# Output blocks stored one by one with the last in the first one's home, activation sums on VectorE only, and layer-norm statistics held until well into the first FFN product

## The chip, the cores and the metric

The kernel runs on one core of one Trainium2 chip. The metric is the device time of one execution in microseconds (us), in the fast state.

Times of one kernel differ by 1 to 2.5 us from execution to execution, once by 5, and much of what is studied here is smaller than that. Beside the time I use one length read from each profiled execution, called **TensorE's stretch** below: from the last attention score matmul ahead of the first steady FFN product (it starts near 33 us) to the start of the kernel's last matmul. It leaves the start-up out.

## The reference, cut to what matters

```python
def _attn_ref(q, k, v):                      # 8 batches, 12 heads, 448 rows, head size 64
    scores = np.matmul(q, k.transpose(0, 1, 3, 2)) / np.sqrt(q.shape[-1])
    attn = np.maximum(scores, 0.0) ** 2 / q.shape[2]
    return np.matmul(attn, v)

def _moe_ref(x, g_ln, w_ch1, w_ch2):         # x: 8 x 448 x 768, inner width 3072
    mu = np.mean(x, axis=-1, keepdims=True)
    var = np.mean((x - mu) ** 2, axis=-1, keepdims=True)
    xn = (x - mu) / np.sqrt(var + 1e-06) * g_ln
    return x + np.maximum(xn @ w_ch1, 0.0) @ w_ch2
```

The attention of a batch comes first; its result x goes through a layer norm and two products with a relu between them.

## The kernel before: the parts that matter

The kernel builds its instruction order itself. `R.add(engines, costs, emit, deps, key)` hands in an operation; where two engines are named, a small model of the chip in the builder gives it to the one that would finish first. The order on each engine is then fixed in the program, and an engine doesn't pass over an instruction that waits: at 490 us of before, ScalarE stood for 1.53 us at a waiting square root while a relu that TensorE needed was behind it. Attention of later batches is laid between FFN matmuls of earlier ones.

Six words for what follows. *ffn_1* is the first FFN product (L929), its relu is L945 on ScalarE or L947 on VectorE. The *second FFN product* of a pair of 128-row tiles is computed from four output blocks (C11, C12 for the first tile, C21, C22 for the second) with seven products P1 to P7 (L1114) instead of eight. These need sums of activations, S1 to S4 (L1074). An *evacuation* (L1128) takes a finished product out of PSUM, multiplies it by 1/std and adds; only then is the PSUM bank free for the next product. *Mean subtraction* (L840) and *gain* (L847 on ScalarE, L849 on VectorE) prepare the input of the next batch's ffn_1.

The activation sums, which the builder may give to VectorE or GpSimd:

```python
def s_op(u, m, name, part, deps):
    ...
    def emit(eng):
        (nc.vector if eng == "DVE" else nc.gpsimd).tensor_sub(o, i0, i1)
    return R.add(("DVE", "POOL"), (540.0, 1700.0), emit, deps, key=-2.9, port=True)
```

`port=True` tells the builder's model that this operation can't run beside one of the other engine that is marked so too. The mean subtraction is not marked:

```python
    subs.append(R.add("DVE", 130.0 + (P if m < 3 else T) * K1 * 1.04,
                      lambda eng, cols=cols, i=i: sub(eng, cols, slice(0, K1), i), [sv], key=-2.0))
```

Evacuations, homes and stores. `e["o", 0]` is a 128 x 768 tile for the first tile's blocks (from two buffers in rotation), `e["o", 1]` a 128 x 384 half tile, of which there is one. `half_free[0]` is the last store out of it:

```python
        if name == "P1":
            evac("c1", 0, lo, r1, False, [o_ring[-N_O]])
        elif name == "P2":
            evac("C11", 0, lo, r1, True, [e["c1"]])
        ...
        elif name == "P5":
            evac("p5", 1, hi, r2, False, [half_free[0]])
        elif name == "P7":
            ev = evac("C22", 1, hi, r2, True, [e["p5"]])
            half_free[0] = store_tile(u, m + 1, hi, ev, False, lambda: e["o", 1])
        elif name == "P3":
            ev = evac("C12", 0, hi, r1, True, [e["c2"], e["C11"]])
            o_ring.append(store_tile(u, m, slice(0, d_model), ev, False, lambda: e["o", 0]))
        else:                                                   # P4
            ev = evac("C21", 1, lo, r2, False, [half_free[0]])
            ...
            half_free[0] = store_tile(u, m + 1, lo, ev, final, lambda: e["o", 1])
```

So C21 needs the half tile that C22 has just used: its evacuation waits for C22's store. Last, the statistics (L790 to L792 on VectorE), their square root on ScalarE (L800) and the reciprocal on VectorE (L802):

```python
            sto = R.add("DVE", 1400.0, stats, [deps_of[m], ops.get(("st0", b))], key=4.0)
        ...
        sq = R.add("ACT", 300.0, root, [ops["st", u, m] for m in ms], key=3.0)
        ops["rstd", b] = R.add("DVE", 150.0, ..., [sq], key=3.0)      # reciprocal
```

## Time and profile before

| | before |
|---|---|
| time, median of 3 | 538.98 us (538.92 to 539.05) |
| span of the profiled execution | 537.3 us |
| TensorE busy | 517.1 us, 96% |
| VectorE / ScalarE / GpSimd busy | 341.8 / 231.3 / 125.2 us |
| TensorE's stretch | 499.43 us |

TensorE is the bound. Two more views belong to the picture. The first is the busy time of each engine in three stretches of before; its columns are the stretch, its length, and for TensorE, its weight loads, VectorE, ScalarE and GpSimd the busy time and the number of instructions; the last three are the clock, the DMA engines' share and GB/s.

```profile
270.00:300.00 30.00, 26.30 (x165) 14.27 (x157) 18.84 (x29) 9.50 (x14) 13.76 (x12) 1.00 1.19 148
400.00:425.00 25.00, 23.20 (x145) 13.01 (x144) 17.15 (x27) 7.46 (x12) 6.11 (x7) 1.00 0.53 107
470.00:500.00 30.00, 29.32 (x162) 15.73 (x161) 9.39 (x23) 10.55 (x20) 1.64 (x1) 1.00 0.24 41
```

The first number after the length is TensorE: it stands still for 3.70, 1.80 and 0.68 us in these three, while it is all but full elsewhere after the start-up. GpSimd is the fifth: it is far busier in the first stretch than its average of 23%.

The durations of the activation sums, by engine (shortest/median/longest in ns, then the first and last start):

```profile
L1074 DVE TENSOR_TENSOR h<-h,x_all x32: 543/550/1561, 199.4 to 524.5; 128x768 bf16<-128x768 bf16 x32
...
L1074 POOL TENSOR_TENSOR h<-h,x_all x4: 1637/1794/1951, 275.5 to 405.7; 128x768 bf16<-128x768 bf16 x4
```

Only four of these 36 run on GpSimd (a fifth sum, of another form, does so at 485.31 us), and two of VectorE's 32 (at 275.97 and 404.59 us) took 1.56 us, almost three times as long as the others. A median alone hides them; the longest tells of them.

### The profile page before, as it was taken

What the parts mean: (1) busy time and instruction counts of PE and PEld (TensorE: products, weight loads), DVE (VectorE), ACT (ScalarE), POOL (GpSimd) and SP (SyncE); (2) the same over time, 40 slices, a digit from 0 to 9 for tenths busy, and PEclk for the clock granted to TensorE, in tenths of its full rate; (3) what the DMA queues carried; (4) which work ended last, traced back from release to release, by engine and by line L of the source; (5) the groups of instructions that cost most, each with busy time, mean ns of one, the idle gap of its engine ahead of it and who ended that gap; (6) DMA issues with size and microseconds to landing.
All of it is one profiled execution on the core that took longest, in us unless ns stands there. A gap on an engine that the chain in (4) does not pass through costs nothing.

```text
span 537.3 us, 9903 instructions
## 1 busy us (share of the span) xinstructions
PE 517.1 (96%) x4128; PEld 278.8 (52%) x4128; DVE 341.8 (64%) x617; ACT 231.3 (43%) x370; POOL 125.2 (23%) x137
## 2 busy tenths in 40 slices
PE   4899999999999999999988999999998999999996
PEld 3444455555564455555544545655555455554564
DVE  5988647448987588665686666746668646633253
ACT  5977611134225653366223663346441565124300
POOL 6411600311460123421172010702222012101000
PEclk9999999999999999999999999999999999999999
DMA  9999999897299004990069900992022400231022
GB/s 187 196 189 195 198 188 165 117 142 134 47 186 187 1 2 68 185 152 1 1 115 159 147 2 1 162 190 52 2 47 71 97 1 1 59 67 23 1 60 59
DMA packets 142680, 51.82 MB, mean 96 GB/s; under 512 B 121510, under 2 KB 139436, under 8 KB 142636
## 3 DMA queue, kind: packets, MB, share of 16 engines
q0 software_dynamic: 81072, 25.50, 45.1%
q1 hardware_dynamic: 55724, 14.79, 17.7%
q10 hardware_dynamic: 5840, 10.92, 7.4%
q8 instruction: 32, 0.52, 0.4%
q14 instruction: 12, 0.10, 0.1%
HBM read 51.91 MB, written 11.01 MB: 117 GB/s over the span
## 4 chain that ended last, share of the span: by engine, by line
PE 90%; DVE 5%; DMA 2%; ACT 1%; issue 1%; SPq 0%; ACTq 0%; DVEq 0%
PE f_ps L929 40%; PE f_ps L1114 20%; PE f_ps L1190 16%; PE sc L586 6%; PE ps L648 5%; DVE a L840 1%; DMA f<-in_k_dram 1%; DVE a L610 1%; DMA out_dram<-o_t 1%; DVE o_t L1128 1%; ACT a L595 1%; PE ps L507 1%; DVE t L365 0%; PE f_ps L909 0%; DVE a L849 0%
## 5 line engine op out<-in xcount | busy, mean ns | idle before, releaser
L929 PE MATMUL f_ps<-a,w 128*128 128x448 bf16 x1134 | 220.9, 353 | 1.8 <-DVE o_t L1128 1.1
L929 PEld LDWEIGHTS <-w 128*128 128x128 bf16 x1134 | 108.3, 98 | 110.3 <-issue 12.5
L595 ACT ACTIVATE a<-sc 128x896 bf16<-128x896 f32 x114 | 99.9, 923 | 85.6 <-PE sc L586 79.8
L945 ACT ACTIVATE h<-f_ps 128x448 bf16<-128x448 f32 (+1 forms) x161 | 86.0, 535 | 103.9 <-PE f_ps L929 102.4
L610 DVE TENSOR_TENSOR a<-a 128x896 bf16<-128x896 bf16 x156 | 99.0, 668 | 3.1 <-ACT a L595 2.8
L1114 PEld LDWEIGHTS <-h 128*128 128x128 bf16 x648 | 62.8, 98 | 48.7 <-issue 7.5
L1114 PE MATMUL f_ps<-w,h 128*128 128x384 bf16 x432 | 75.6, 326 | 4.4 <-DVE o_t L1128 4.4
L597 DVE TENSOR_SCALAR a<-sc 128x896 bf16<-128x896 f32 x45 | 48.9, 1087 | 24.5 <-PE sc L586 24.4
L1190 PE MATMUL f_ps<-w,h 128*128 128x384 bf16 x372 | 62.1, 326 | 0.0
L586 PE MATMUL sc<-t 64*64 64x448 bf16 x672 | 48.4, 365 | 3.3 <-ACT a L595 1.6
L1190 PEld LDWEIGHTS <-h 128*128 128x128 bf16 x372 | 36.0, 98 | 25.2 <-issue 1.7
L739 POOL TENSOR_TENSOR sum_t<-sum_t,xT_all 128x384 f32<-128x384 f32 (+2 forms) x25 | 20.4, 815 | 99.0 <-ACT xT_all L363 99.0
L1074 DVE TENSOR_TENSOR x_all<-h 128x768 bf16<-128x768 bf16 x18 | 9.9, 562 | 38.5 <-ACT h L945 38.5
L1128 DVE SCALAR_TENSOR_TENSOR o_t<-f_ps,r_t,x_all 128x384 f32<-128x384 f32 x36 | 22.1, 615 | 18.8 <-PE f_ps L1114 14.9
L586 PEld LDWEIGHTS <-t 64*64 64x64 bf16 x672 | 17.6, 106 | 26.5 <-issue 20.1
L737 POOL TENSOR_TENSOR sum_t<-xT_all 128x384 f32<-128x384 bf16 (+2 forms) x13 | 9.2, 720 | 88.9 <-ACT xT_all L363 88.8
L648 PE MATMUL ps<-a,v_t 64*64 64x448 bf16 x552 | 29.8, 350 | 0.0
L847 ACT ACTIVATE a<-a,g_sb 128x448 bf16<-128x448 bf16 x27 | 16.1, 657 | 31.2 <-DVE a L840 30.1
L1128 DVE SCALAR_TENSOR_TENSOR o_t<-f_ps,r_t,o_t 128x384 f32<-128x384 f32 x27 | 16.6, 615 | 19.4 <-PE f_ps L1114 19.2
L363 ACT CAST xT_all<-ps 128x768 bf16<-128x768 f32 (+2 forms) x33 | 20.2, 622 | 20.1 <-PE ps L648 18.3
L401 POOL DMA_DIRECT2D t<-in_q_dram x12 | 19.3, 1774 | 36.1 <-DMA t<-t 34.6
L648 PEld LDWEIGHTS <-v_t 64*64 64x64 bf16 x672 | 19.7, 107 | 13.4 <-issue 2.8
(91 smaller groups left out, 420.2 us busy)
## 6 DMA issues: line engine op xcount, KB each, us to landing
out_dram<-o_t ACTq DMA_DIRECT2D x38, 192.0 KB, 4.7
v_t<-in_v_dram POOLq DMA_DIRECT2D x16, 336.0 KB, 6.3
w<-in_moe_w_ch_dram POOLq DMA_DIRECT2D x4, 1152.0 KB, 40.0
t<-in_q_dram POOLq DMA_DIRECT2D x12, 336.0 KB, 8.3
t<-in_k_dram POOLq DMA_DIRECT2D x12, 336.0 KB, 10.5
out_dram<-o_t ACTq DMA_DIRECT2D x35, 96.0 KB, 2.2
w<-in_moe_w_ch_dram POOLq DMA_DIRECT2D x4, 768.0 KB, 19.2
w<-in_moe_w_ch_dram POOLq DMA_DIRECT2D x1, 1536.0 KB, 29.2
```

What stands on the lines that cost most here:

```text
L363: nc.scalar.copy(o, i)
L586: nc.tensor.matmul(sc[rows_of(half), r, :S], qkT[b][rows_of(r), 1, s * NPER + pn, rows_of(half)], qT[:, :, pn, rows_of(half)], start=True, ...
L595: nc.scalar.activation(attn[n, s], st[0][:, :, :S], Act.Relu, scale=rc2)
L597: nc.vector.tensor_scalar(attn[n, s], st[0][:, :, :S], rc2, 0.0, op0=Alu.mult, op1=Alu.max)
L610: nc.vector.tensor_mul(attn[n, s], attn[n, s], attn[n, s])
L648: nc.tensor.matmul(av_st[n][half][rows_of(hh)], vt[b][rows_of(half), 2 * pn + hh, s * D:(s + 1) * D], attn[n, s][rows_of(half), hh, :], st ...
L739: nc.gpsimd.tensor_add(s0, s0, x0)
L929: nc.tensor.matmul(st[0], w1[:, ki, ni * P:(ni + 1) * P], xc[b][:, ki, :], start=(i == 0), stop=(i == K1 - 1))
L945: nc.scalar.activation(o, st[0][:, c], Act.Relu)
L1114: nc.tensor.matmul(e["ps", bank], a(k), w(k), start=new and k == 0, stop=k == KH - 1, skip_group_check=True)
L1128: nc.vector.scalar_tensor_tensor(o, e["ps", bank], r, o if more else xm[u, m + tile_n][:, cols], op0=Alu.mult, op1=Alu.add)
L1190: nc.tensor.matmul(o_st["ps"], stat(u, m, ki), w, start=(i == 0), stop=(i == len(ks) - 1))
```

## The change

It has three parts. The sums are given to VectorE alone. Each output block is stored when it is done, and C21, the last, goes into C11's home in the 128 x 768 tile, which C11's own early store has freed. And for all but the first pair of batches, the statistics wait for the fifth relu of the same batch's ffn_1 (index 4), the square root for the fifteenth (index 14). It is this relu that takes ffn_1 out of PSUM; the recorded texts call it ffn_1's evacuation.

```diff
-            sto = R.add("DVE", 1400.0, stats, [deps_of[m], ops.get(("st0", b))], key=4.0)
+            sto = R.add("DVE", 1400.0, stats, [deps_of[m], ops.get(("st0", b)), later("h", b, 4) if u > 0 else None], key=4.0)
 ...
-        sq = R.add("ACT", 300.0, root, [ops["st", u, m] for m in ms], key=3.0)
+        sq = R.add("ACT", 300.0, root, [ops["st", u, m] for m in ms] + [later("h", b, 14) if u > 0 else None], key=3.0)
 ...
-        return R.add(("DVE", "POOL"), (540.0, 1700.0), emit, deps, key=-2.9, port=True)
+        return R.add("DVE", 570.0, emit, deps, key=-2.9, port=True)
 ...
-                elif key in ("p5", "C21"):
+                elif key == "p5":
 ...
-                o = e["o", 1] if tile_n else e["o", 0][:, cols]
+                o = e["o", 1] if key in ("p5", "C22") else e["o", 0][:, cols]
 ...
-            evac("C11", 0, lo, r1, True, [e["c1"]])
+            ev = evac("C11", 0, lo, r1, True, [e["c1"]])
+            e["C11 out"] = store_tile(u, m, lo, ev, False, lambda: e["o", 0][:, lo])
 ...
-            o_ring.append(store_tile(u, m, slice(0, d_model), ev, False, lambda: e["o", 0]))
+            e["C12 out"] = store_tile(u, m, hi, ev, False, lambda: e["o", 0][:, hi])
 ...
-            ev = evac("C21", 1, lo, r2, False, [half_free[0]])
+            ev = evac("C21", 1, lo, r2, False, [e["C11 out"]])
 ...
-            half_free[0] = store_tile(u, m + 1, lo, ev, final, lambda: e["o", 1])
+            o_ring.append([e["C12 out"], store_tile(u, m + 1, lo, ev, final, lambda: e["o", 0][:, lo])])
```

## The prediction

> **What bounds the kernel now.** I read the page first. Its busy line and the first line of its chain of waits say that TensorE sets the time:
>
> ```profile
> PE 517.1 (96%) x4128; PEld 278.8 (52%) x4128; DVE 341.8 (64%) x617; ACT 231.3 (43%) x370; POOL 125.2 (23%) x137
> PE 90%; DVE 5%; DMA 2%; ACT 1%; issue 1%; SPq 0%; ACTq 0%; DVEq 0%
> ```
>
> The change removes no matmul, so it can only win what TensorE stands still. The second number of the second line is not that amount: the chain runs through VectorE and a store for most of 276 to 293 us, yet TensorE works through much of that stretch. So I went to TensorE's timeline and listed every wait after 30 us (before that, the start-up, the built order of the changed kernel is the same). Five rows carry nearly all of it; the bracket at the end is the idle time before the row and who ended it:
>
> ```profile
> 281.30 2.11 PE L1114 MATMUL f_ps<-w,h 128*128 128x384 bf16 x12 [1.80 <-DVE o_t L1128]
> 286.12 2.11 PE L1114 MATMUL f_ps<-w,h 128*128 128x384 bf16 x12 [0.76 <-DVE o_t L1128]
> 293.25 6.97 PE L929 MATMUL f_ps<-a,w 128*128 128x448 bf16 x36 [1.13 <-DVE o_t L1128]
> ...
> 409.91 2.11 PE L1114 MATMUL f_ps<-w,h 128*128 128x384 bf16 x12 [1.80 <-DVE o_t L1128]
> ...
> 490.95 14.91 PE L929 MATMUL f_ps<-a,w 128*128 128x448 bf16 x78 [0.68 <-ACT h L945]
> ```
>
> Matmul ends are modelled, so I size each by the cadence instead: rows of 12 start 1.95 us apart, 0.1625 us a matmul; the 448-column ones 0.189 us. The row before 281.30 began at 278.84 with three matmuls, so it could have gone on at 279.33: lost 1.97. Likewise 283.24 + 12 x 0.1625 = 285.19 against 286.12: 0.93. 290.80 + 6 x 0.189 = 291.93 against 293.25: 1.32. 407.45 + 3 x 0.1625 = 407.94 against 409.91: 1.97. 477.62 + 66 x 0.189 = 490.09 against 490.95: 0.86. Sum: **7.05 us**. There is one more of 0.32 us at 428.94.
>
> Why VectorE was late: its own timeline and GpSimd's, same stretch.
>
> ```profile
> 275.97 1.56 DVE L1074 TENSOR_TENSOR h<-h,x_all 128x768 bf16<-128x768 bf16 x1
> 277.46 3.25 DVE L840 TENSOR_TENSOR a<-xT_all,sum_t 128x768 bf16<-128x768 bf16 x2
> 280.64 0.60 DVE L1128 SCALAR_TENSOR_TENSOR o_t<-f_ps,r_t,o_t 128x384 f32<-128x384 f32 x1
> ...
> 283.49 2.05 DVE L849 TENSOR_SCALAR a<-a,g_sb 128x448 bf16<-128x448 bf16 x3
> 285.47 0.60 DVE L1128 SCALAR_TENSOR_TENSOR o_t<-f_ps,r_t,x_all 128x384 f32<-128x384 f32 x1
> ...
> 292.58 0.62 DVE L1128 SCALAR_TENSOR_TENSOR o_t<-f_ps,r_t,x_all 128x384 f32<-128x384 f32 x1 [3.69 <-DMA out_dram<-o_t]
> ```
> ```profile
> 275.49 3.55 POOL L1074 TENSOR_TENSOR h<-h,x_all 128x768 bf16<-128x768 bf16 x2 [1.37 <-PE f_ps L1114]
> ```
>
> While GpSimd does two of the four activation sums (L1074), VectorE's own sum takes 1.56 us where its median is 0.55, and one of the two mean subtractions (L840) takes 2.39 where it is 0.95 elsewhere. The evacuation that frees the PSUM bank comes behind them, at 280.64. 404 to 410 us is the same picture (sums 3.55, L840 3.26). Later the gain multiplications (L849) take 2.05 for three, where 0.81 is usual (412.11), while GpSimd issues loads, and the evacuation at 285.47 is late. At 292.58 the last block of the tile pair waits for the half-tile buffer, whose store was issued at 287.33 and took 5.05 us to land (the chain gives both); the median of such a 96 KB store is 2.2, but the q and k loads fill the DMA engines until 291.6. The fifth wait is another: ScalarE runs in order, and its square root for the statistics stood waiting for VectorE's statistics, which had waited for the transposed x:
>
> ```profile
> 486.62 0.56 DVE L790 BATCH_NORM_STATS2 st<-x_all 128x6 f32<-128x384 bf16 x1 [7.04 <-DMA x_all<-xT_all]
> ...
> 490.17 0.30 ACT L800 ACTIVATE r_t<-mv_t,eps_sb 128x4 f32<-128x4 f32 x1 [1.53 <-DVE mv_t L792]
> ```
>
> **What the Trainium skill says.** "SBUF — State Buffer", section "Who interferes with whom": a VectorE instruction with two SBUF inputs and a GpSimd instruction that reads SBUF lock each other out, and the loser blocks for the whole instruction. The trace agrees: 1.56 and 2.39 us above. The same section says that two-input operations do not keep GpSimd from writing DMA descriptors (marked as inferred there) while tensor_scalar in a fast mode can collide. Agrees: L840 beside load issues has a median of 0.95 us as without them, one L849 took 1.34 instead of 0.33. "GPSIMD Engine Reference", "Engine selection": two-input elementwise work is about 2x slower on GpSimd; here a median of 1.79 against 0.55, 3.3x. "DMA: Bandwidth & Descriptors", "Anatomy of one DMA": about 2 us are fixed, whatever the size; the 2.2 us of 96 KB agree, so splitting stores doesn't shorten them much, only starts them sooner.
>
> **The change part by part.**
>
> *Sums on VectorE alone.* Five go from GpSimd to VectorE (two at 275, two at 404, one at 485): + 5 x 0.55 = 2.75 us on VectorE, - 8.7 on GpSimd. Walking the new order of VectorE from 275.44 with durations of this trace: evacuation to 276.06, two sums to 277.1, one L840 to 278.0, the evacuation that held TensorE 278.0 to 278.6 (was 280.64), two sums to 279.6, L840 to 280.5, the next evacuation to 281.1, where TensorE needs it at 281.3; L840 to 282.0, evacuation to 282.6 (needed at 283.24). So all evacuations are ahead: 1.97 + 0.93 saved here, 1.97 at 409. GpSimd goes on to the load issues at 274.6 instead of 279.0 and is done near 281, ahead of the gains (283), so the 0.93 should not come back.
>
> *Last block in the first one's home.* It now waits for the store of the first block of the same pair, issued near 278.7 in the walk; even with 5 us it lands at 284, and the last block's evacuation is due at 287.4. Saved: 1.32. Cost: 9 pairs x 2 = 18 more store issues on ScalarE, about 0.55 each, 9.9 us in all, in an engine 43% busy whose waits for TensorE alone are 80 us at L595 and 102 at L945: beside other work. At the very end nothing is won: the last evacuation follows the last matmul either way (533.20), and the page's span ends 3.5 us after that, mostly the last store's landing.
>
> *Statistics held.* The statistics of six batches (the later three pairs), 1.26 us for each tile, only move later; the square root comes after the 15th evacuation of ffn_1, near 495 us in the last batch, when the statistics (from 486.6, four tiles and two sums, about 6 us) are done. Saved: 0.86. They also leave the stretch in which the gains are due.
>
> *Side effects of the new order.* The rows of the built programs differ also in this: 9 gains and 4 relus of attention go from ScalarE to VectorE and 3 relus of FFN back, one square to GpSimd. VectorE: 9 x 0.33 + 4 x 1.09 - 3 x 0.62 - 0.62 + 2.75 = + 7.6; less what the lock cost it (2 x 2.45 + 1.0), net about + 2 us of 342. TensorE's order differs in one attention visit that comes 24 matmuls later, at the place of the 0.32 wait: I count 0.3 for it.
>
> Sum: 7.05 + 0.3 = 7.35 saved at best. For new small waits (VectorE margins of 0.2 us in the walk, the square on GpSimd, later squares on VectorE behind the statistics) I take off 0.65, a choice, not a reading. 538.98 - 6.7 = **532.3 us**.
>
> **The rivals.** (1) *VectorE becomes the bound at the mean subtraction.* It takes two more sums where it was the late one. For: margins of 0.2 us. Against: without the lock it gains 2.45 and pays 1.1. If it happened, half of the 4.9 us there stays: about 535. (2) *The wait for a store moves*, to the first block's store or to ScalarE's issue queue: loads begin 4 us sooner and slow all stores to 5 us. For: the 5.05 seen. Against: 3.4 us of slack. Time then about 533.6. (3) *Held statistics make VectorE late in ffn_1*: 3 to 4 tiles of 1.26 us fall among attention squares; a late square holds an attention visit. Six batches x 0.4 would give 2.4 us back: about 535. (4) *Hidden anyway*: the waits only move to the next wait for TensorE's input. Against: after each, TensorE runs on without a gap for tens of us.
>
> **Range and chances.** The floor is all 7.35 saved, 531.6, and a bit of noise; the ceiling is one rival in full. 531.0 to 535.2. Faster by 2% would need 10.8 us, more than TensorE loses in all: 0.01. Slower by 2% needs a new wait in every batch: 0.01. Within 2%: 0.98.
>
> **What would show it.** TensorE's timeline without the five brackets, and busy 517 of a span near 530.6. GpSimd without L1074, busy near 118. L1074 and L840 on VectorE without values over 1 us. Last blocks without a wait for the store. ScalarE's square root without 1.53 of waiting. It is wrong if TensorE shows new brackets released by VectorE's evacuations, by ScalarE's relus or by a store, or if VectorE's L840 and L849 are still stretched by load issues.

## The result, and the profile after

| | before | after |
|---|---|---|
| time, median of 4, in the same rounds | 539.01 us (538.92 to 539.26) | 532.45 us (531.90 to 532.75) |
| span of the profiled execution | 537.3 us | 530.5 us |
| TensorE's stretch | 499.43 us | 492.50 us |
| VectorE / ScalarE / GpSimd busy | 341.8 / 231.3 / 125.2 us | 344.9 / 224.6 / 118.2 us |

The ratio of the times is 0.9876, with a 95% interval of 0.9859 to 0.9894. Ratios here are the mean time of one kernel's fast runs over that of the other's of the same rounds, so not quite the ratio of the medians. The change wins 1.2%, which is within 2%.

First the busy time in the same three stretches as before (the columns are the same):

```profile
270.00:300.00 30.00, 30.00 (x220) 16.61 (x213) 20.40 (x39) 11.93 (x19) 10.24 (x10) 1.00 1.39 170
400.00:425.00 25.00, 24.71 (x181) 13.46 (x179) 19.03 (x38) 10.71 (x16) 1.55 (x2) 1.00 0.31 72
470.00:500.00 30.00, 30.00 (x163) 15.75 (x162) 9.10 (x21) 12.70 (x24) 0.00 (x0) 1.00 0.23 33
```

TensorE is full but for 0.29 us in the second. The kernel is some 7 us ahead of before by the last stretch, so the stretches don't hold quite the same work; for the sizes I use the cadence. Then the busy line and the chain of waits of after:

```profile
PE 516.0 (97%) x4128; PEld 278.4 (52%) x4128; DVE 344.9 (65%) x631; ACT 224.6 (42%) x360; POOL 118.2 (22%) x133
PE 94%; DVE 3%; DMA 1%; ACT 1%; issue 0%; SPq 0%; ACTq 0%; DVEq 0%
```

The number of matmuls is unchanged, and the share of the chain that runs through VectorE and DMA fell from 7% to 4%. Next TensorE's timeline, at the places that answer to the five rows of before, and one more; a bracket would be idle time ahead of the row:

```profile
279.18 2.11 PE L1114 MATMUL f_ps<-w,h 128*128 128x384 bf16 x12
...
283.08 2.11 PE L1114 MATMUL f_ps<-w,h 128*128 128x384 bf16 x12
...
287.76 6.42 PE L929 MATMUL f_ps<-a,w 128*128 128x448 bf16 x33
...
403.61 2.11 PE L1114 MATMUL f_ps<-w,h 128*128 128x384 bf16 x12
...
422.63 0.38 PE L586 MATMUL sc<-t 64*64 64x448 bf16 x4 [0.29 <-ACT a L595]
...
479.72 12.46 PE L929 MATMUL f_ps<-a,w 128*128 128x448 bf16 x65
```

No bracket is left in the first stretch, none at 403.61 (409.91 of before), and the ffn_1 row at 479.72 runs on through the place where the square root had stopped it. The square root itself, on ScalarE, now stands behind more relus and waits for nothing:

```profile
489.12 0.29 ACT L800 ACTIVATE r_t<-mv_t,eps_sb 128x4 f32<-128x4 f32 x1
```

The bracket at 422.63 is the attention wait that before had at 428.94 (0.32 us there); it stayed. By the cadence it is larger than its bracket: attention rows otherwise start 0.19 us apart, and 0.46 us are lost here, 0.48 in before. VectorE and GpSimd in the first stretch:

```profile
275.82 1.01 DVE L1074 TENSOR_TENSOR h<-h,x_all 128x768 bf16<-128x768 bf16 x2
276.76 0.95 DVE L840 TENSOR_TENSOR a<-xT_all,sum_t 128x768 bf16<-128x768 bf16 x1
277.63 0.61 DVE L1128 SCALAR_TENSOR_TENSOR o_t<-f_ps,r_t,o_t 128x384 f32<-128x384 f32 x1
...
287.18 0.62 DVE L1128 SCALAR_TENSOR_TENSOR o_t<-f_ps,r_t,x_all 128x384 f32<-128x384 f32 x1 [1.33 <-PE f_ps L1114]
```
```profile
274.45 3.21 POOL L401 DMA_DIRECT2D t<-in_q_dram  x2 [0.50 <-issue]
276.94 3.96 POOL L401 DMA_DIRECT2D t<-in_k_dram  x2
```

Two sums now take together less than the one did that met GpSimd, the subtraction is back at 0.95, and the evacuation that held TensorE starts at 277.63 instead of 280.64. The last row of VectorE is the last block's evacuation: what ended its idle time is now the product itself, not a store. GpSimd goes from its attention sums straight to the loads.

### The profile page after: what moved, and what is told of

The parts are those of the page before. It is cut to its first block, busy times and chain, and to the rows that moved or that the text cites. A ratio compares the mean times of both kernels' runs of the same rounds, so it can differ in the third digit from the quotient of the medians.

```text
span 530.5 us, 9925 instructions
## 1 busy us (share of the span) xinstructions
PE 516.0 (97%) x4128; PEld 278.4 (52%) x4128; DVE 344.9 (65%) x631; ACT 224.6 (42%) x360; POOL 118.2 (22%) x133
## 4 chain that ended last, share of the span: by engine, by line
PE 94%; DVE 3%; DMA 1%; ACT 1%; issue 0%; SPq 0%; ACTq 0%; DVEq 0%
PE f_ps L929 41%; PE f_ps L1114 23%; PE f_ps L1191 16%; PE sc L586 6%; PE ps L648 5%; DMA f<-in_k_dram 1%; DVE a L610 1%; ACT a L595 1%; DVE a L858 1%; DVE t L365 1%; PE ps L507 1%; PE ps L710 0%; PE slot L819 0%; PE f_ps L648 0%; DVE xT_all L365 0%
## 5 line engine op out<-in xcount | busy, mean ns | idle before, releaser
L595 ACT ACTIVATE a<-sc 128x896 bf16<-128x896 f32 x110 | 96.7, 923 | 89.4 <-PE sc L586 80.0
L945 ACT ACTIVATE h<-f_ps 128x448 bf16<-128x448 f32 (+1 forms) x164 | 87.8, 535 | 105.6 <-PE f_ps L929 103.9
L597 DVE TENSOR_SCALAR a<-sc 128x896 bf16<-128x896 f32 x49 | 53.2, 1086 | 22.1 <-PE sc L586 22.0
L1128 DVE SCALAR_TENSOR_TENSOR o_t<-f_ps,r_t,x_all 128x384 f32<-128x384 f32 x36 | 22.1, 614 | 17.6 <-PE f_ps L1114 17.5
L1207 DVE SCALAR_TENSOR_TENSOR o_t<-f_ps,r_t,x_all 128x384 f32<-128x384 f32 x20 | 12.2, 612 | 26.9 <-PE f_ps L1191 26.9
L1074 DVE TENSOR_TENSOR h<-h 128x768 bf16<-128x768 bf16 x18 | 9.8, 571 | 27.2 <-ACT h L945 27.2
```

Source lines behind the costliest of these rows:

```text
L595: nc.scalar.activation(attn[n, s], st[0][:, :, :S], Act.Relu, scale=rc2)
L597: nc.vector.tensor_scalar(attn[n, s], st[0][:, :, :S], rc2, 0.0, op0=Alu.mult, op1=Alu.max)
L945: nc.scalar.activation(o, st[0][:, c], Act.Relu)
L1128: nc.vector.scalar_tensor_tensor(o, e["ps", bank], r, o if more else xm[u, m + tile_n][:, cols], op0=Alu.mult, op1=Alu.add)
```

## The experiments

All kernels gave correct results, and all the new ones were timed in five rounds, 4 to 6 executions each; the row of after repeats the result above. The third column is TensorE's stretch less before's 499.43 us. Kernels are compared only within the same rounds.

| run | TensorE's stretch | against before | median time (before) | ratio, 95% interval |
|---|---|---|---|---|
| sums_only | 495.49 | -3.94 | 534.61 (538.75) | 0.9928, 0.9913 to 0.9942 |
| store_only | 498.00 | -1.43 | 537.64 (538.75) | 0.9978, 0.9966 to 0.9990 |
| stats_only | 498.91 | -0.52 | 538.42 (538.88) | 0.9984, 0.9966 to 1.0001 |
| *after* | 492.50 | -6.93 | 532.45 (539.01) | 0.9876, 0.9859 to 0.9894 |
| pool_reads | 494.80 | -4.63 | 534.47 (538.75) | 0.9922, 0.9909 to 0.9935 |
| pool_writes | 492.50 | -6.93 | 532.66 (538.75) | 0.9881, 0.9866 to 0.9895 |
| pool_reads_late | 496.75 | -2.68 | 536.78 (539.47) | 0.9947, 0.9935 to 0.9960 |
| before_port | 498.58 | -0.85 | 538.24 (539.47) | 0.9986, 0.9963 to 1.0009 |
| no_store | 493.15 | -6.28 | 533.36 (538.88) | 0.9887, 0.9868 to 0.9907 |
| split_same_home | 493.77 | -5.66 | 534.08 (538.88) | 0.9897, 0.9878 to 0.9915 |
| no_stats | 494.07 | -5.36 | 534.52 (538.88) | 0.9909, 0.9892 to 0.9926 |
| after_root | 492.52 | -6.91 | 533.50 (539.47) | 0.9885, 0.9872 to 0.9897 |
| hold6 | 491.92 | -7.51 | 531.83 (539.47) | 0.9858, 0.9845 to 0.9871 |

### Is it the read lock between VectorE and GpSimd?

My theory: with a sum on GpSimd, the two engines lock each other out, so VectorE's own sums and subtractions stretch and the evacuations come late. The rival: VectorE just has a better order now, or GpSimd reaches its loads earlier. **pool_reads** takes after as it is and lets GpSimd do two additional subtractions that read SBUF, with results that nobody uses; **pool_writes** lets it fill as much memory twice instead, which only writes. VectorE's order is that of after in both.

```diff
+        if name == "P1" and m == 5 and u < B // 2 - 1:
+            def extra(eng):
+                dead = qkT[b + 1][:, 0, 0:6, :]
+                i = w1[:, 0, 0:768].rearrange("p (o c) -> p o c", c=P)
+                nc.gpsimd.tensor_sub(dead, i, i)          # pool_writes: memset of dead, 0:12
+            for _ in range(2):
+                R.add("POOL", 1750.0, extra, [op], key=-2.95)
```

> The changed kernel, VectorE's order untouched, with two added GpSimd subtractions of 128x768 bf16 (they read weights and write a dead buffer) where the kernel before had two sums on GpSimd, in the two stretches (275 and 400 us). Port theory: VectorE's sums and mean subtractions stand blocked as before (single ones of 1.5 to 2.4 us instead of 0.55 and 0.95), TensorE's waits for VectorE's evacuations come back, 1.5 to 2.5 us at each place: 535.5 to 537.5 us, some 4 over the changed kernel's 532.45. Rival (the new order of VectorE's queue is what helps, not the absence of GpSimd work): within 0.3 us of 532.45, VectorE's durations as in the changed kernel.

> The same with two GpSimd memsets of 128x1536 bf16 into the dead buffer: GpSimd is busy and its load issues come later, but nothing of SBUF is read. Port theory with reads alone in the way of two-input operations: VectorE's sums stay at 0.55 and mean subtractions at 0.95 us; only the gains (L849), now beside the later load issues, may be stretched by about 1 us in the first stretch: 532.4 to 533.5 us. Rival (any GpSimd work there blocks VectorE, or the later loads are what cost time): as the run with reads, 535 us or more.

In pool_writes, GpSimd's and VectorE's timelines are:

```profile
274.64 2.81 POOL L1137 MEMSET t<- 128x1536 bf16 x2
```
```profile
276.58 1.02 DVE L1074 TENSOR_TENSOR h<-h,x_all 128x768 bf16<-128x768 bf16 x2
277.51 0.95 DVE L840 TENSOR_TENSOR a<-xT_all,sum_t 128x768 bf16<-128x768 bf16 x1
```

GpSimd writes until 277.45, beside two attention squares (1.15 us together, as in after) and two sums (1.02 against 1.01), which are not stretched; it is done before the subtraction starts, so that one was not tested against writes. The loads begin at 277.40 instead of 274.45, and TensorE's stretch is the same to 0.01 us. So neither a busy GpSimd nor later loads cost TensorE anything here. The later loads are not without any effect: the four gains at 283.22, beside the last of them, took 1.48 us where 1.07 is usual, within the slack. In pool_reads the sums are stretched and TensorE's wait is back:

```profile
276.23 1.76 DVE L1074 TENSOR_TENSOR h<-h,x_all 128x768 bf16<-128x768 bf16 x2
```
```profile
279.44 2.11 PE L1114 MATMUL f_ps<-w,h 128*128 128x384 bf16 x12 [0.61 <-DVE o_t L1128]
```

It cost 2.30 us of stretch. That was less than expected, and the trace says why: the two reads ran from 273.39, some 2 us before GpSimd's sums in the kernel before, so part of them fell on attention squares (two took 2.42 us instead of 1.15), which had time to spare. **pool_reads_late** sets a memset ahead of the two reads, so that they run at the old sums' time:

```diff
+            def pad(eng):
+                nc.gpsimd.memset(qkT[b + 1][:, 0, 0:18, :], 0.0)
-            for _ in range(2):
+            for fn in (pad, extra, extra):
```

> As pool_reads, whose GpSimd work turned out to start 2 us sooner than the kernel before's sums (it has no true wait for the product), so that half of it met the squares: now a memset of 128x2304 goes ahead of the two subtractions and moves them to about 275.4 to 279 us, where the sums had stood. Port theory: the two sums and one mean subtraction are now blocked for most of 3.5 us, and TensorE loses about 2 us at each of the two places: 535.5 to 537 us, more than pool_reads' 534.5. If the port costs no more than pool_reads showed: 534 to 535.

GpSimd, VectorE and TensorE in pool_reads_late:

```profile
275.36 3.44 POOL L1137 TENSOR_TENSOR t<-w 128x768 bf16<-128x768 bf16 x2
```
```profile
275.19 2.29 DVE L1074 TENSOR_TENSOR h<-h,x_all 128x768 bf16<-128x768 bf16 x2
277.40 2.21 DVE L840 TENSOR_TENSOR a<-xT_all,sum_t 128x768 bf16<-128x768 bf16 x1
279.54 0.60 DVE L1128 SCALAR_TENSOR_TENSOR o_t<-f_ps,r_t,o_t 128x384 f32<-128x384 f32 x1
```
```profile
280.20 2.11 PE L1114 MATMUL f_ps<-w,h 128*128 128x384 bf16 x12 [1.49 <-DVE o_t L1128]
```

A hit: 4.25 us of stretch, of which the matmul cadence shows 1.65 + 0.39 here and the same near 407 us. The same VectorE order with reads beside it loses about as much as the sums' move alone won (3.94, below); with writes beside it, nothing. The lock on reads is the cause of the two waits of 1.97 us, and the size of its cost depends on what VectorE was doing when it was locked.

The remaining 0.17 us of the 4.25 stand at 286.62, and they bear on the wait of 0.93 us at 286 in before, which has no experiment of its own. The loads of pool_reads_late are issued as late as those of before (278.75 to 285.21 us), and four gains beside them took 1.67 us instead of 1.07; in before, three took 2.05 instead of 0.81. So this second collision, of gains with load issues, comes back with the late loads, but only a small part of the wait does. Where the rest went, to the place of the gains in after's order of VectorE or to the smaller stretching, is not separated.

If the lock is the whole of it, the builder only has to know that the mean subtraction is subject to it. **before_port** marks it so in the kernel before and changes nothing else:

```diff
-    lambda eng, cols=cols, i=i: sub(eng, cols, slice(0, K1), i), [sv], key=-2.0))
+    lambda eng, cols=cols, i=i: sub(eng, cols, slice(0, K1), i), [sv], key=-2.0, port=True))
```

> The kernel before with one word more: the mean subtraction is told to the kernel's own scheduler as an operation that takes the shared port. It then puts the sums of both stretches on VectorE of its own accord, but three of the four behind the evacuation of the third product. Port theory: no blocked operation any more, but the second sum comes about 1.5 us late for TensorE at each place, so some 2 us of the 4.87 are won: 536.5 to 537.5 us. Rival (assignment alone decides, not the order): as sums_only, 534.6.

A miss: 0.85 us of stretch, and a time that can't be told from before's. The lock is gone: no sum is on GpSimd in this stretch. But three of the four sums now stand behind subtractions, and TensorE waits for a sum itself; and the last block's wait for a store became worse. TensorE, then a piece of the chain of waits:

```profile
280.40 1.15 PE L1114 MATMUL f_ps<-w,h 128*128 128x384 bf16 x6 [0.71 <-DVE h L1074]
```
```profile
284.70 6.54 DMA out_dram<-o_t
```

By the cadence the waits near 280 and 408 us fell from 1.97 to 0.87 each and the one at 286 went (together -3.12); the wait for the store grew from 1.30 to 2.87 (+1.57), the one for the square root from 0.84 to 1.54 (+0.69). Sum -0.86, as measured. Freed of one wait, TensorE ran earlier into the next two, which are set by a transfer (the store was issued 2.6 us earlier than in before, but took 6.54 us to land instead of 5.05) and by transposed x. That is why the three parts belong together.

### Each part alone

sums_only, store_only and stats_only take one part of the diff into the kernel before.

> The kernel before with the sums on VectorE alone, nothing else. My reading of the waits: 1.97 + 0.93 + 1.97 = 4.87 us less, 538.98 to 534.1 us; the wait for the half tile's store and the one for the square root stay. Rival (VectorE becomes the bound when it takes the sums): no more than 2.5 us less, 536.5 or more.

> The kernel before with blocks stored one by one and the last in the first one's home, nothing else. My reading: the wait at 293 us, 1.32 us, goes: 537.7 us. Rival (hidden anyway, or 18 more store issues on ScalarE cost what is won): 538.7 or more.

> The kernel before with the statistics and their square root held, nothing else. My reading: the wait at 490 us, 0.86 us, goes: 538.1 us, and the square root shows no wait for VectorE's statistics. Rival (held statistics make VectorE late among the attention squares): new waits, 538.9 us or more.

The sums alone remove 4.86 us of waits (1.97 + 0.93 + 1.97), the store wait shrinks by 0.31, and 1.25 come back at the square root, whose wait grew from 0.84 to 2.10: -3.92, measured -3.94. That is why the time came out 0.5 us above what was expected. This is ScalarE's square root in sums_only:

```profile
485.48 0.30 ACT L800 ACTIVATE r_t<-mv_t,eps_sb 128x4 f32<-128x4 f32 x1 [2.78 <-DVE mv_t L792]
```

It waits 2.78 us where it waited 1.53 in the kernel before: two sums, one of which GpSimd used to do and one of which followed the statistics, now stand among the statistics on VectorE (0.9 us), and transposed x comes 0.3 us later against TensorE. The store part alone took its 1.30 and, by chance of timing, 0.15 at the root: as expected. The statistics alone took the root's 0.84, but the wait for the store grew by 0.19 (to 1.48), so about half a microsecond was left; in time (interval 0.9966 to 1.0001) this part can't be told from before. The three alone sum to -5.89, together they are -6.93: 1.04 us are won only because each part also meets what another would have made worse.

### Is it the early store, or the home?

**no_store** is after with the old stores and homes. **split_same_home** keeps after's early single stores, but lets C21 use the half tile again.

```diff
# split_same_home against after
-                elif key == "p5":
+                elif key in ("p5", "C21"):
-                o = e["o", 1] if key in ("p5", "C22") else e["o", 0][:, cols]
+                o = e["o", 1] if tile_n else e["o", 0][:, cols]
-            ev = evac("C21", 1, lo, r2, False, [e["C11 out"]])
+            ev = evac("C21", 1, lo, r2, False, [half_free[0]])
-            o_ring.append([e["C12 out"], store_tile(u, m + 1, lo, ev, final, lambda: e["o", 0][:, lo])])
+            half_free[0] = store_tile(u, m + 1, lo, ev, final, lambda: e["o", 1])
+            o_ring.append([e["C11 out"], e["C12 out"]])
```

> The changed kernel with the stores and the half tile as they were. My reading: the last block's evacuation near 287 us waits again for the half tile's store, which lands slowly beside the q and k loads, and TensorE waits about 1 us: 533.3 to 533.8 us. Rival (with VectorE early, the store is early enough too): within 0.4 us of 532.45.

> The changed kernel with the blocks still stored one by one, but the last block back in the half tile. If the home is what matters: as no_store, about 1 us slower than 532.45, with the wait for a store at the last block's evacuation. If the early, smaller stores are what matters: within 0.4 us of 532.45.

no_store lost 0.65 us of stretch, somewhat less than the expected 1; its time lies in the expected band. split_same_home lost more, 1.27. VectorE and TensorE of the latter:

```profile
288.87 0.62 DVE L1128 SCALAR_TENSOR_TENSOR o_t<-f_ps,r_t,x_all 128x384 f32<-128x384 f32 x1 [3.66 <-DMA out_dram<-o_t]
```
```profile
289.54 2.81 PE L929 MATMUL f_ps<-a,w 128*128 128x448 bf16 x14 [1.11 <-DVE o_t L1128]
```

So smaller, earlier stores do nothing for C21. C22's store even lands later, 4.8 us after its issue instead of 4.1 in no_store; that the additional store ahead of it is the reason is likely, not shown. The home decides, because it makes C21 wait for a store issued almost 6 us sooner. And that margin turned out to be needed. The store of C11 in after, issued at 278.27 and 278.78 (shortest/median/longest from issue to landing):

```profile
L1229 ACTq DMA_DIRECT2D out_dram<-o_t x2: 473/818/1164, 278.3 to 278.8; - x2
...
DMA to landing us min/median/max: 6.7/6.7/6.7
```

It landed at 285.45, 1.7 us before C21's evacuation at 287.18. A second half tile would have told home and order apart more directly, but it needs 1.5 KB more of each partition; it was not run.

### What in the held statistics matters?

**no_stats** is after without the third part; **after_root** holds the square root only; **hold6** holds the statistics until the seventh evacuation instead of the fifth.

```diff
# no_stats against after: both waits out; after_root: only the first one out
-    ... stats, [deps_of[m], ops.get(("st0", b)), later("h", b, 4) if u > 0 else None], key=4.0)
+    ... stats, [deps_of[m], ops.get(("st0", b))], key=4.0)
-    ... root, [ops["st", u, m] for m in ms] + [later("h", b, 14) if u > 0 else None], key=3.0)
+    ... root, [ops["st", u, m] for m in ms], key=3.0)
# hold6 against after
-    ... later("h", b, 4) if u > 0 else None ...
+    ... later("h", b, 6) if u > 0 else None ...
```

> The changed kernel without the held statistics. My reading: the wait for the square root near 484 us returns, 0.8 us, perhaps more where the statistics fall among the gains: 533.2 to 533.8 us. Rival (it was POOL's late sum or luck of the order): within 0.3 us of 532.45.

> The changed kernel with the square root still held until the 15th evacuation, but the statistics themselves not held. If the wait was ScalarE standing at the square root, this half is the whole effect: 532.2 to 532.8 us, no wait at 484. If the statistics' place in VectorE's queue matters too: 533 us or more, with new waits where gains or evacuations stand behind statistics.

> A try at a faster one: the changed kernel with the statistics held until the 7th instead of the 5th evacuation of ffn_1, so that VectorE is free to take one of the attention relus near 421 us, where TensorE still loses 0.94 us (0.64 + 0.30) because ScalarE does all of them while VectorE does statistics. If so: 531.5 us and no wait there. If VectorE is then late elsewhere: 532.4 or more.

no_stats lost 1.57 us of stretch, more than the 0.86 that I had taken for this part, and its time of 534.52 lies above the expected band. ScalarE and TensorE in no_stats:

```profile
484.58 0.30 ACT L800 ACTIVATE r_t<-mv_t,eps_sb 128x4 f32<-128x4 f32 x1 [2.35 <-DVE mv_t L792]
```
```profile
485.36 1.86 PE L929 MATMUL f_ps<-a,w 128*128 128x448 bf16 x9 [1.50 <-ACT h L945]
```

In after_root the statistics run on VectorE as early as in no_stats, with the two sums among them (480.63 to 485.08 us), but the square root stands later in ScalarE's order:

```profile
489.51 0.29 ACT L800 ACTIVATE r_t<-mv_t,eps_sb 128x4 f32<-128x4 f32 x1
```

It has no wait, and TensorE's stretch is 492.52 us, after's to 0.02. Its median of 533.50 alone would have said otherwise: it lies on the wrong side of the expected band. But before ran 0.46 us slower in that call too, its ratio of 0.9885 agrees with after's, and its profiled execution had a start-up of 33.64 us, 0.37 longer than after's, and a last store that took 2.75 us to land instead of 2.41; the two make the 0.7 us by which its span is longer. The stretch decides: of the third part only the held root changes anything in it.

hold6 has the best ratio of all, 0.9858, though its interval overlaps after's. The mechanism that was expected is in the trace. The attention wait at 422 us is gone in TensorE's timeline, and VectorE's timeline shows a relu of attention before the statistics, which start at 421.26:

```profile
420.25 1.09 DVE L597 TENSOR_SCALAR a<-sc 128x896 bf16<-128x896 f32 x1 [0.46 <-PE sc L586]
```

In after, VectorE does statistics from 420.33 on, so ScalarE does two attention relus in a row, which TensorE waits for. With the hold two relus of ffn_1 later the builder gives one attention relu to VectorE. TensorE's stretch is 0.58 us shorter, not the 0.94 expected: the wait was of 0.46 us by the cadence. Whether it beats after in time by that much is likely, but not settled by these runs.

## Why the prediction was right

**The sum.** 6.7 us were predicted; the medians differ by 6.56 and the ratio makes 0.0124 x 539.0 = 6.7. In the profiled executions TensorE's stretch is 6.93 us shorter, the start-up was 0.14 shorter, and the end from the last matmul's start was 0.29 longer, which makes the 6.8 us by which the spans differ. That longer end is in most runs with single stores (4.75 to 4.78 us; two of them had 4.99 and 5.10) against 4.46 to 4.53 in the runs without; the prediction had no term for it. The last store lands 3.4 us after the last matmul's start in before and after alike, so the 0.29 lie behind all stores, among the program's closing instructions; why they are longer was not looked for.

**The five waits**, 7.05 us, all went: 7.00 by the cadence of all rows. **The attention wait**, 0.3, did not go: the row at 422.63 loses 0.46 us by the cadence, before's lost 0.48. The prediction had sized this one by its bracket and the other five by the cadence, so its term was too small as well as unearned. **The allowance** of 0.65 for new waits was not used up: only 0.07 is missing from the 7.00. The two small misses cancel, which is luck; the total is better than its small terms.

**The walk of VectorE** put the three evacuations at 278.0, 280.5 and 282.0; they came at 277.63, 279.96 and 281.35. It added full durations, where successive instructions overlap by about 0.08 us. Its order was right.

**The lock** was shown for the two waits of 1.97 us, not only argued: reads of the same size at the same time bring the wait back, writes don't. What the prediction left out is that removing the lock alone is worth little if the sums end up behind the subtractions (before_port).

**The store**: the saving was right, but the margin was not. "Even with 5 us it lands at 284" was 285.45, as the store took 6.66 us while the earlier loads filled the queues. The slack was 1.7 us instead of 3.4. Rival 2 was nearer than I had thought.

**The statistics**: the term of 0.86 was right for the kernel before, too small for its place in this change. There the root would have waited for two sums more, and the part saves 1.6 us (no_stats). In the sum of the whole it made no difference, because what the sums would have given back was never counted either. What held the time was the root's place on ScalarE; the statistics' own hold did nothing in TensorE's stretch (after_root), and none of the loss that rival 3 feared came.

**The signs.** One sign that the prediction had named as proving it wrong did appear: gains on VectorE are still stretched beside load issues (1.36 us at 155.1, 1.14 at 219.4 and 0.85 at 342.1 of after, where 0.33 is usual; after gives VectorE 30 gains, before 21). TensorE shows no wait at these places, so the sign was named too broadly.

**Rival 1** did not come about either: in after, subtractions take 0.958 us at the longest. **Rival 4**, that a wait only moves to the next one, was refuted for the whole change, but holds for its parts: sums_only gave back 1.25 us at the root and before_port 2.26 at the store and the root.

## What to carry to other kernels

Count what the bounding engine stands still, wait by wait, by the cadence of its instructions: it gave this result to a few tenths of a us, while busy shares and the chain of waits did not. Then ask what the next wait in line is when one is removed; a transfer or an in-order engine waiting for late data takes back what was won unless it is moved too. An operation given to an idle engine is not free if it reads what the busy one reads through, and a small operation that waits in an engine's fixed order should be placed where its input is surely ready.

## What the Trainium skill lacked or had wrong

- "SBUF — State Buffer", "Who interferes with whom": its rule that a VectorE instruction with two SBUF inputs collides with GpSimd reads and not with writes held in these runs. What it lacks is what that costs in a pipeline. Two reads of 128 x 768 in each of two stretches took 2.30 or 4.25 us of TensorE, depending on 2 us of placement (pool_reads, pool_reads_late); two memsets of 2.81 us took 0.00 (pool_writes).
- "GPSIMD Engine Reference", "Engine selection", gives about 2x for two-input operations. A bf16 subtraction of 128 x 768 took 1.64 us on GpSimd while VectorE was idle for all but the last 0.3 us (485.31 us of before), against 0.55 on VectorE: 3.0x. The row names no type, and the page measures the ratio for fp32 alone; what it lacks is the figure for bf16.
- "DMA: Bandwidth & Descriptors", "Anatomy of one DMA", gives a fixed 2 us for a transfer issued by GpSimd. The prediction carried it over to a 96 KB store issued by ScalarE's queue, which agrees with it as a median (2.2 us), but such a store took 6.7 us while GpSimd's loads were in flight. A figure for a store beside such loads is lacking, and a buffer's margin has to be sized by it.
- No page that this study drew on has a figure for what one small waiting instruction costs in an engine's fixed order: a square root of 0.30 us held ScalarE for 2.35 us and TensorE for 1.50 (no_stats), and nothing at all when placed 5 us later (after_root).
